# Weight loads of the retention stage: from SyncE's queue to ScalarE's

## The chip, the cores and the metric

The kernel runs on one core of one Trainium2 chip. What counts is the device time of one execution in microseconds (us); lower is better. Engines are named as the profile names them: PE (TensorE, the matrix multiplies; PEld its weight loads), DVE (VectorE), ACT (ScalarE), POOL (GpSimd) and SP (SyncE, which here only starts transfers). A transfer (DMA) is issued by one engine's instruction stream, stands in that engine's queue, and is carried out by 16 DMA engines that all queues share.

## The reference

Three blocks follow one another: a retention (linear attention with decay), a soft mixture of experts, and a two-layer MLP.

```python
# retention: q, k, v are (4, 8, 768, 64)
gamma = 1.0 - 2.0 ** (-5.0 - np.arange(H))
for t in range(S):
    state = gamma * state + einsum('bhd,bhe->bhde', k[:, :, t], v[:, :, t])
    y[:, :, t] = D ** -0.5 * einsum('bhd,bhde->bhe', q[:, :, t], state)
x = y as (3072 tokens, 512)
# soft mixture of experts: phi (512, 32), w1 (8, 512, 1024), w2 (8, 1024, 512)
logits = x @ phi
slot_input = softmax(logits, axis=0).T @ x
slot_out = relu(slot_input @ w1[e]) @ w2[e]          # per expert e, 4 slots each
x = softmax(logits, axis=1) @ slot_out
# MLP: w_in (512, 2048), w_out (2048, 512)
h = x @ w_in
out = (h * sigmoid(1.702 * h)) @ w_out
```

## The kernel before

The retention is computed in 24 chunks of 128 tokens (four batches of six chunks). For each chunk three tensors come from memory: `ktv` (512 KB: the transposed k and the plain v side by side), `qt` (256 KB, transposed q) and, for 12 of the chunks, `kt` (256 KB, plain k; the chunks in `KTP` get it from a transpose on PE, copied out by ACT at L222, and the last chunk of a batch needs none). Each has three buffers that are used in turn.

The loop over i (its body starts at L876) works on several chunks at a time. Iteration i does `stage_a(i)` (scores `sc`, L210, from q and k of chunk i), `stage_v(i)` (POOL scales v), `stage_b(i-1)` (output `y` from the state at L255 and from the scores at L259, then the new state `st` at L267, which ACT copies to `s_sb` at L269), `stage_c(i-2)` (a transpose `xp`, which ACT copies to `x` at L291). Every fourth iteration adds the logits of a group of four chunks and the copies of them on ACT (L337 to L321), the next one the group's first softmax steps.

Loads are issued in the same iteration: the halves of expert weights (below), `load_b(i+1)` for k, and `load_a(i+2)` for `ktv` and q of chunk i+2. The buffer of q that `load_a(i+2)` fills is that of chunk i-1, and its last reader is `y` at L255 in `stage_b(i-1)`. The whole program stands under a manual schedule: each engine runs its instructions in the order in which the code lists them, and SP does so too, so that it may run ahead of the others as far as its waits allow.

Expert weights are cut into 32 pieces of 1 MB. During the retention 17 of them are loaded, in 34 halves of 512 KB (`load_half`, L120), into buffers that nothing has used before (`wp` and `wq`; one of them held `ktv` of chunk 2). The loop issues three halves in iteration 1 and then one or two in each iteration up to 22, by `min(2 * (NW + NQ), 2 + i * 2 * (NW + NQ) // (NI - I0))` with NW + NQ = 17. The other 15 pieces are loaded behind the retention (`load_piece`, L136, and two halves), when buffers of the retention are free; their first users are the matrix multiplies `hp` (L488) and `eo` (L513).

All loads of the loop are issued by SP. ACT issues two loads of constants at the very start, POOL two more. SP's and ACT's issues together draw on eight completion semaphores in turn, in program order, so that each issue waits until the eighth one before it has landed.

Of the kernel before, what the change touches and what calls it, by code (L numbers as in the profile page):

```python
# [33 lines left out]
NW = 14  # L34
# [15 lines left out]
def retention_soft_moe_mlp(  # L50
# [13 lines left out]
    nc = tc.nc  # L64
# [3 lines left out]
    def pool(stack, name, bufs, **kw):  # L68
        e = ctx.enter_context(ExitStack())
        kw.setdefault("reuse_waits", "tile")  # L70
        if "space" not in kw:
            kw["side"] = "left" if stack is left else "right"
        t = e.enter_context(tc.tile_pool(name=name, bufs=bufs, **kw))
        return t, e
# [4 lines left out]
    wp, _ = pool(left, "wp", NW)  # L79
    sm, sm_e = pool(right, "sm", 2)  # L80
    xx, xx_e = pool(right, "xx", 5)
    wq, wq_e = pool(left, "wq", NQ)
# [34 lines left out]

    half = []

    def load_half(pool):  # L120
        if half:
            t, src = half.pop()
            nc.sync.dma_start(out=t[:, 2:4], in_=src[:, 2:4])
            return
        kind, e, k = pieces.pop()
        t = pool.tile([P, 4, 512], F32, tag="w", name=f"{kind}_{e}_{k}")
        src = (w1 if kind == "w1" else w2)[e, k].rearrange("p (j f) -> p j f", j=4)
        nc.sync.dma_start(out=t[:, 0:2], in_=src[:, 0:2])
        W[kind, e, k] = t
        half.append((t, src))  # L130

# [42 lines left out]
    def load_a(i):  # L174
        if i < NI:
            src = ktv[i].rearrange("p (a t) -> p a t", a=2)
            if i == 2:
                early.append(wp.tile([P, 4, 512], F32, tag="w", name="early"))
                ktv_t[i] = early[0][:, 0:2]
            else:  # L180
                ktv_t[i] = wt(f"ktv{i % 3}", [P, 2, 512], f"ktv{i}")
            if i < 2:
                nc.sync.dma_start(out=ktv_t[i][:, 0], in_=src[:, 0])
            else:
                nc.sync.dma_start(out=ktv_t[i], in_=src)
            qt_t[i] = wt(f"qt{(i + 1) % 3}", [P, NP, P], f"qt{i}")
            nc.sync.dma_start(out=qt_t[i], in_=qt[i].rearrange("p (a t) -> p a t", a=NP))
# [4 lines left out]
    def load_b(i):  # L192
        if i < NI and i % NC < NC - 1:
            if i == 3:
                t = early[0][:, i].rearrange("p (h d) -> p h d", h=H)
            else:
                t = wt(f"kt{(i - i // NC) % 3}", [P, H, D], f"kt{i}")
            if i not in KTP:
                nc.sync.dma_start(out=t, in_=kt[i].rearrange("p (h d) -> p h d", h=H))
            kt_t[i] = t  # L200
# [3 lines left out]
    def stage_a(i):  # L204
        q_, kv = qt_t[i], ktv_t[i]
        kT = kv[:, 0].rearrange("p (a t) -> p a t", a=NP)
        sc = [ps.tile([P, NP, P], F32, tag=f"sc{hh}", name=f"sc{hh}_{i}") for hh in range(2)]
        for a in range(NP):
            for hh in range(2):
                mm(sc[hh][:, a, :], lhsT=kT[hh * D:(hh + 1) * D, a, :], rhs=q_[hh * D:(hh + 1) * D, a, :],  # L210
                   start=True, stop=True)
        pt = [wt(f"pt{hh}{i % 2}", [P, NP, P], f"pt{hh}_{i}") for hh in range(2)]
        for hh in range(2):
            nc.vector.tensor_tensor(  # L214
                out=pt[hh], in0=sc[hh], in1=mask[:, None, :].to_broadcast([P, NP, P]), op=ALU.mult
            )
        p_t[i] = pt
        if i in KTP and i % NC < NC - 1:
            kp = ps.tile([P, NP, P], F32, tag="m", name=f"kp{i}", bufs=3)
            for a in range(NP):  # L220
                nc.tensor.transpose(kp[:, a, :], kT[:, a, :], ident)
            nc.scalar.copy(out=kt_t[i].rearrange("p h d -> p (h d)"), in_=kp.rearrange("p a t -> p (a t)"))  # L222

    def stage_v(i):
        c = i % NC
        v_ = ktv_t.pop(i)[:, 1].rearrange("p (h d) -> p h d", h=H)
        vt = wt(f"vt{i % 2}", [P, H, D], f"vt{i}")
        nc.gpsimd.tensor_tensor(
            out=vt, in0=v_, in1=vs[:, c, :, None].to_broadcast([P, H, D]), op=ALU.mult
        )  # L230
        vt_t[i] = vt
        if c == 0:
            tb_t[i] = tab
        else:
            tb_t[i] = wt("tb", [P, NP, P], f"tb{i}")
            nc.gpsimd.tensor_tensor(
                out=tb_t[i], in0=tab, in1=gsc[:, :, c, None].to_broadcast([P, NP, P]), op=ALU.mult
            )
# [3 lines left out]
    def stage_b(i):  # L242
        c = i % NC
        q_, vt, pt = qt_t.pop(i), vt_t.pop(i), p_t.pop(i)
        y = ps.tile([P, 2, 512], F32, tag="y", name=f"y{i}")

        def out_(a, hh):
            o = hh ^ (a & 1)
            return y[o * D:(o + 1) * D, a % 2, P * (a // 2):P * (a // 2) + P]

        if c > 0:
            for a in range(NP):
                for hh in range(2):
                    r = slice(hh * D, (hh + 1) * D)
                    mm(out_(a, hh), lhsT=s_sb[r, a, :], rhs=q_[r, a, :], start=(a < 2), stop=False,  # L255
                       skip_group_check=True)
        for a in range(NP):
            for hh in range(2):
                mm(out_(a, hh ^ (a & 1)), lhsT=vt[:, 2 * a + (hh ^ (a & 1)), :], rhs=pt[hh ^ (a & 1)][:, a, :],  # L259
                   start=(c == 0 and a < 2), stop=True, skip_group_check=True)  # L260
        if c < NC - 1:
            if c == 0:
                st_p[0] = ps.tile([P, NP, D], F32, tag="st", name=f"st{i}")
            st, k_ = st_p[0], kt_t.pop(i)
            for a in range(NP):
                for hh in range(2):
                    mm(st[hh * D:(hh + 1) * D, a, :], lhsT=k_[:, 2 * a + hh, :], rhs=vt[:, 2 * a + hh, :],  # L267
                       start=(c == 0 and a == 0), stop=True, skip_group_check=True)
            nc.scalar.copy(out=s_sb, in_=st)  # L269
        xT = xx.tile([P, NP, P], F32, tag="xT", name=f"xT{i}")  # L270
        nc.vector.tensor_tensor(
            out=xT.rearrange("p (s k) t -> p k s t", k=2), in0=y[:, :, 0:2 * P].rearrange("p k (s t) -> p k s t", s=2),
            in1=tb_t.pop(i).rearrange("p (s k) t -> p k s t", k=2), op=ALU.mult,
        )
        xT_t[i] = xT

    def stage_c(i, split=False):
        xp = ps.tile([P, DM], F32, tag="m", name=f"xp{i}", bufs=3)
        for a in range(NP):
            nc.tensor.transpose(xp[:, a * P:(a + 1) * P], xT_t[i][:, a, :], ident)  # L280
        x_t[i] = xp
        if not split:
            stage_c2(i)
# [15 lines left out]
    def stage_g1(g, part=False):  # L299
        if part in (True, False):  # L300
            lp = logits(g)
            if part:
                return lp
        else:
            lp = part
        softmax_stats(g, lp)
# [547 lines left out]
    with tc.manual_schedule():  # L854
# [18 lines left out]
        loaded = 0  # L873
        ex_t = {}
        for i in range(NI + 2):
            if i == 2:  # L876
                stage_b(1)
            if i < NI:
                stage_a(i)
                stage_v(i)  # L880
                while i > 0 and loaded < min(2 * (NW + NQ), 2 + i * 2 * (NW + NQ) // (NI - I0)):
                    load_half(wp if loaded < 2 * NW else wq)
                    loaded += 1
                load_b(i + 1)
                load_a(i + 2)
            if i >= 8 and i % 4 == 0 and i < NI:
                ex_t[i // 4 - 2] = row_softmax(i // 4 - 2)
            if i >= 9 and i % 4 == 1 and i < NI:
                row_norm(i // 4 - 2, ex_t.pop(i // 4 - 2))
            if 1 <= i <= NI and i != 2:  # L890
                stage_b(i - 1)
            if i >= 2:
                n = i - 1
                g = n // 4 - 1
                if i < NI + 1:
                    stage_c(i - 2)
                else:
                    lp = stage_g1(g, True)
                    stage_c(i - 2, True)
                    softmax_stats(g, lp)  # L900
                    combine1()
                    last_z = stage_g2(g)
                    stage_c2(i - 2)
                if n % 4 == 0 and i <= NI:
                    stage_g1(g)
                if n % 4 == 1 and n > 4:
                    stage_g2(g)
                if n % 4 == 2 and 4 < n < 22:
                    stage_g3(g)
# [337 lines left out]
```

## Time and profile before

| | before |
|---|---|
| median of 3 runs | 450.64 us (448.06 to 453.56) |
| the profiled execution | 451.76 us |
| its span | 450.0 us |
| PE busy | 433.1 us (96% of the span) |
| DVE, ACT, POOL busy | 333.4, 205.3, 47.9 us |
| moved by DMA | 92.38 MB, 79.16 MB read from memory |
| q1, the queue of nearly all transfers | 27248 packets, 91.24 MB |

The retention takes the first 109 us or so of the span. The span is the time from the first to the last instruction; the rest of an execution's time lies around it. PE's granted clock is 0.999 of full speed in this execution. A busy share is an average over the span; what ends a wait in one stage is read from that stage.

### The profile page before, as it was taken

The numbers are of one execution on the slowest core, as the hardware profiler recorded it, in microseconds if no ns is written. First come the engines' busy times: TensorE is split into PE (matmuls) and PEld (weight loads), VectorE is DVE, ScalarE is ACT, GpSimd is POOL, SyncE is SP. The second block draws the span as 40 slices with busy tenths as digits, with TensorE's granted clock in tenths as the row PEclk, the third lists the DMA queues.
The fourth block names the chain that finished last, engine by engine and source line by source line (L and its number), as shares of the span: only waits on it lengthen the run. The fifth ranks groups of instructions, "written<-read, shape, count | busy, mean of one in ns | idle before, by whom it ended". The sixth has DMA issues, their size and how long they took to land.

```text
span 450.0 us, 9917 instructions
## 1 busy us (share of the span) xinstructions
PE 433.1 (96%) x4105; PEld 359.9 (80%) x4105; DVE 333.4 (74%) x600; ACT 205.3 (46%) x351; POOL 47.9 (11%) x53
## 2 busy tenths in 40 slices
PE   8799998999999989999999999999999999999996
PEld 5687876877533367788888889999999999999995
DVE  2345665756456587987979689897797797988984
ACT  2232232322220166474656655655555555565530
POOL 3353543343100000000000000000000000000000
PEclk9999999999999999999999999999999999999999
DMA  8999999999899968687555502001301401311012
GB/s 300 407 365 408 389 371 407 344 407 325 328 411 411 380 228 281 182 299 268 181 194 188 184 5 94 1 1 47 129 14 47 141 1 49 140 48 46 23 74 93
DMA packets 27661, 92.38 MB, mean 205 GB/s; under 512 B 2864, under 2 KB 4288, under 8 KB 23264
## 3 DMA queue, kind: packets, MB, share of 16 engines
q1 hardware_dynamic: 27248, 91.24, 55.1%
q8 instruction: 32, 0.52, 0.5%
q10 hardware_dynamic: 288, 0.36, 0.3%
q0 software_dynamic: 80, 0.15, 0.1%
q14 instruction: 13, 0.11, 0.1%
HBM read 79.16 MB, written 12.58 MB: 204 GB/s over the span
## 4 chain that ended last, share of the span: by engine, by line
PE 81%; DMA 12%; DVE 3%; ACT 1%; issue 1%; POOL 1%; SPq 0%; DVEq 0%; POOLq 0%; ACTq 0%
PE P L730 35%; PE acc L667 18%; DMA qt<-qt_dram 10%; PE sc L210 4%; PE hb L696 4%; PE hp L488 3%; PE y L259 3%; PE eo L513 3%; PE y L255 2%; PE P L840 2%; PE xp L280 1%; PE op L370 1%; PE h L644 1%; DMA ktv_first<-ktv_dram 1%; PE st L267 1%
## 5 line engine op out<-in xcount | busy, mean ns | idle before, releaser
L691 DVE TENSOR_TENSOR forms<-forms 128x256 f32<-128x256 f32 (+1 forms) x93 | 47.6, 512 | 22.3 <-ACT forms L698 21.0
L698 ACT ACTIVATE forms<-hb 128x512 f32<-128x512 f32 x62 | 37.2, 599 | 54.7 <-PE hb L696 34.9
L667 PE MATMUL acc<-wo_hl,gh 128*128 128x512 f32 x192 | 59.8, 394 | 0.4 <-ACT gh L646 0.4
L730 PE MATMUL P<-bh,la 128*128 128x256 f32 x208 | 59.0, 284 | 0.0
L730 PE MATMUL P<-bl,ha 128*128 128x256 f32 x208 | 58.8, 283 | 0.0
L730 PE MATMUL P<-bh,ha 128*128 128x256 f32 x208 | 58.7, 282 | 0.0
L214 DVE TENSOR_TENSOR pt<-sc,ca_t 128x512 f32<-128x512 f32 x44 | 28.3, 685 | 24.5 <-PE sc L210 24.5
L730 PE MATMUL P<-bh,hs 128*128 128x256 f32 x156 | 44.1, 283 | 0.0
L730 PE MATMUL P<-bh,ls 128*128 128x256 f32 x156 | 44.1, 282 | 0.0
L730 PE MATMUL P<-bl,hs 128*128 128x256 f32 x156 | 44.0, 282 | 0.0
L667 PEld LDWEIGHTS acc<-wo_hl,gh 128*128 128x128 f32 x192 | 35.4, 188 | 8.1 <-issue 0.6
L730 PEld LDWEIGHTS P<-bl,ha 128*128 128x128 f32 x208 | 39.4, 189 | 1.2
L730 PEld LDWEIGHTS P<-bh,ha 128*128 128x128 f32 x208 | 39.4, 190 | 0.0
L730 PEld LDWEIGHTS P<-bh,la 128*128 128x128 f32 x208 | 39.4, 189 | 0.1
L691 DVE TENSOR_TENSOR la<-forms,ha 128x1024 fp32r<-128x1024 f32 x31 | 37.9, 1223 | 0.0
L667 PE MATMUL acc<-wo_hl,gl 128*128 128x512 f32 x96 | 37.4, 394 | 0.3 <-DVE gl L654 0.3
L714 ACT CAST ha<-forms 128x1024 fp32r<-128x1024 f32 x31 | 32.6, 1053 | 6.5 <-DVE forms L691 5.6
L646 ACT ACTIVATE gh<-h 128x512 fp32r<-128x512 f32 x30 | 18.0, 601 | 33.0 <-PE h L644 24.2
L714 ACT CAST hs<-forms 128x768 fp32r<-128x768 f32 x31 | 26.0, 839 | 10.1 <-DVE forms L691 7.5
L730 PEld LDWEIGHTS P<-bl,hs 128*128 128x128 f32 x156 | 29.5, 189 | 1.2
L210 PEld LDWEIGHTS sc<-qt,ktv 64*128 64x128 f32 x320 | 19.6, 187 | 13.1 <-issue 9.2
L210 PE MATMUL sc<-qt,ktv 64*128 64x128 f32 x320 | 23.2, 284 | 6.6 <-DMA qt<-qt_dram 6.6
(224 smaller groups left out, 925.2 us busy)
## 6 DMA issues: line engine op xcount, KB each, us to landing
w<-w_dram SPq DMA_DIRECT2D x36, 512.0 KB, 7.7
w<-w_dram SPq DMA_DIRECT2D x14, 1024.0 KB, 8.3
ktv<-ktv_dram SPq DMA_DIRECT2D x20, 512.0 KB, 8.3
wi<-w_in_dram SPq DMA_DIRECT2D x7, 1024.0 KB, 5.5
wo<-w_out_dram SPq DMA_DIRECT2D x7, 1024.0 KB, 4.9
parts<-stage SPq DMA_DIRECT2D x24, 256.0 KB, 2.9
pt<-parts SPq DMA_DIRECT2D x6, 1024.0 KB, 4.8
qt<-qt_dram SPq DMA_DIRECT2D x21, 256.0 KB, 6.5
```

What stands on the lines that cost most here:

```text
L210: mm(sc[hh][:, a, :], lhsT=kT[hh * D:(hh + 1) * D, a, :], rhs=q_[hh * D:(hh + 1) * D, a, :], start=True, stop=True)
L214: nc.vector.tensor_tensor(out=pt[hh], in0=sc[hh], in1=mask[:, None, :].to_broadcast([P, NP, P]), op=ALU.mult)
L259: mm(out_(a, hh ^ (a & 1)), lhsT=vt[:, 2 * a + (hh ^ (a & 1)), :], rhs=pt[hh ^ (a & 1)][:, a, :], start=(c == 0 and a < 2), stop=True, ski ...
L488: mm(hp[32 * j:32 * j + 32, :], lhsT=slotT[:, k, SPE * (j // 2):SPE * (j // 2) + NS], rhs=w[:, j, :], start=(k == 0), stop=(k == KDM - 1))
L513: mm(op[32 * j:32 * j + 32, :], lhsT=hT[:, kk, 32 * j:32 * j + 32], rhs=w[:, j, :], start=(kk == 0), stop=(kk == 3))
L646: nc.scalar.activation(out=gh, in_=hp, func=AF.Gelu_apprx_sigmoid)
L667: mm(acc[t], lhsT=g[:, t * P:(t + 1) * P], rhs=w, start=f == f0 and n == 0, stop=f == f1 and n == 2)
L691: nc.vector.tensor_tensor(out=out_, in0=a, in1=b_, op=op)
L696: mm(PB["h"], lhsT=gst[:, f * P:(f + 1) * P], rhs=cT[:, 512 * b:512 * b + 512], start=True, stop=True)
L698: nc.scalar.activation(out=t[:, 3 * a:3 * a + 2].rearrange("p s d -> p (s d)"), in_=PB["h"], func=AF.Gelu_apprx_sigmoid)
L714: nc.scalar.copy(out=AH[n, k], in_=FT[0][:, c0:c1])
L730: mm(PB[p][:, t], lhsT=g[:, c], rhs=w, start=r == span_[b][0] and t == 0 and i == 0, stop=r == span_[b][1] - 1 and i == 2, skip_group_chec ...
```

## The change

`load_half` gets a second argument, the engine that issues the load. The loop of the retention passes `nc.scalar`, so the 34 halves that it loads are issued by ACT, at the same place of the program. The two halves that are loaded behind the retention pass none and stay with SP, as do all loads of chunks. Sizes, buffers and order in the program are the same.

```diff
-    def load_half(pool):
+    def load_half(pool, q=None):
         if half:
             t, src = half.pop()
-            nc.sync.dma_start(out=t[:, 2:4], in_=src[:, 2:4])
+            (q or nc.sync).dma_start(out=t[:, 2:4], in_=src[:, 2:4])
             return
         kind, e, k = pieces.pop()
         t = pool.tile([P, 4, 512], F32, tag="w", name=f"{kind}_{e}_{k}")
         src = (w1 if kind == "w1" else w2)[e, k].rearrange("p (j f) -> p j f", j=4)
-        nc.sync.dma_start(out=t[:, 0:2], in_=src[:, 0:2])
+        (q or nc.sync).dma_start(out=t[:, 0:2], in_=src[:, 0:2])
...
                 while i > 0 and loaded < min(2 * (NW + NQ), 2 + i * 2 * (NW + NQ) // (NI - I0)):
-                    load_half(wp if loaded < 2 * NW else wq)
+                    load_half(wp if loaded < 2 * NW else wq, nc.scalar)
                     loaded += 1
```

## Rows read from the trace of the kernel before

**Rows 1.** Windows: stretch, length, busy us of engines, clock, DMA share, GB/s.

```profile
core 0: us, PE busy (x) PEld busy (x) DVE busy (x) ACT busy (x) POOL busy (x), PEclk, DMA share, GB/s
4.00:8.00 4.00, 3.97 (x24) 2.06 (x22) 0.59 (x1) 0.00 (x0) 0.00 (x0) 1.00 1.02 362
8.00:18.40 10.40, 7.99 (x124) 6.77 (x124) 4.66 (x8) 2.99 (x6) 6.19 (x6) 1.00 1.03 410
...
72.10:90.60 18.50, 17.47 (x302) 14.01 (x302) 11.15 (x23) 5.33 (x14) 7.32 (x8) 1.00 1.01 370
...
125.00:150.00 25.00, 25.00 (x220) 8.66 (x216) 15.82 (x54) 3.75 (x7) 0.95 (x1) 1.00 1.01 413
```

**Rows 2.** DMA view, all queues, 18.4 to 109 us.

```profile
DMA packets 11744, 34.88 MB, mean 385 GB/s; under 512 B 1302, under 2 KB 1302, under 8 KB 11656
```

**Rows 3.** Waits of PE, 0 to 125 us: total us, times, longest.

```profile
PE sc L210 <- DMA qt<-qt_dram: 6.6, 6, 1.8
...
PE y L255 <- ACT s_sb L269: 0.5, 1, 0.5
```

**Rows 4.** Chain of waits: start us, us, what; transfers of q.

```profile
9.95 8.45 DMA qt<-qt_dram
...
46.56 7.25 DMA qt<-qt_dram
...
101.19 7.78 DMA qt<-qt_dram
```

**Rows 5.** Lines L187 at 5.1, L136 at 120.4, L187 to 125 us, each with landings.

```profile
L187 SPq DMA_DIRECT2D qt_first<-qt_dram x1: 524/524/524, 5.1 to 5.1; - x1
...
DMA to landing us min/median/max: 5.9/5.9/5.9
...
L136 SPq DMA_DIRECT2D w<-w_dram x1: 327/327/327, 120.4 to 120.4; - x1
...
DMA to landing us min/median/max: 4.8/4.8/4.8
...
L187 SPq DMA_DIRECT2D qt<-qt_dram x21: 327/328/664, 9.9 to 101.2; - x21
...
DMA to landing us min/median/max: 4.1/6.4/8.4
```

**Rows 6.** DMA issues, 0 to 109 us: count, KB each, median us to landing.

```profile
w<-w_dram SPq DMA_DIRECT2D x34, 512.0 KB, 7.6
ktv<-ktv_dram SPq DMA_DIRECT2D x20, 512.0 KB, 8.3
qt<-qt_dram SPq DMA_DIRECT2D x21, 256.0 KB, 6.5
kt<-kt_dram SPq DMA_DIRECT2D x12, 256.0 KB, 7.9
```

**Rows 7.** Timeline of SP: start us, us, what.

```profile
5.92 0.33 SPq L128 DMA_DIRECT2D w<-w_dram  x1
...
9.58 0.33 SPq L185 DMA_DIRECT2D ktv<-ktv_dram  x1
...
101.57 0.43 SPq L123 DMA_DIRECT2D w<-w_dram  x1
```

**Rows 8.** Waits of SP's queue, 0 to 110 us: total us, times, longest.

```profile
SPq L187 <- PE y L255: 36.6, 17, 4.1
...
SPq L185 <- POOL vt_first L228: 1.1, 1, 1.1
```

**Rows 9.** Timeline of ACT: start us, us, what, idle before it.

```profile
10.53 0.59 ACT L222 COPY kt_first<-kp 128x512 f32<-128x512 f32 x1 [1.94 <-PE kp L221]
12.03 0.37 ACT L269 COPY s_sb<-st 128x256 f32<-128x256 f32 x1 [0.91 <-PE st L267]
...
99.48 0.59 ACT L291 COPY x<-xp 128x512 f32<-128x512 f32 x1
...
105.47 0.25 ACT L321 COPY lT<-lp 128x128 f32<-128x128 f32 x1
```

## The prediction, made before the changed kernel was run

> **What bounds the kernel now.** The change touches only loads of the retention, the first 109 us, so I read that stretch. First the table of windows, cut where PE waited [rows 1]. The reader is to see two columns. PE is busy nearly all the time (17.47 of 18.50 us in 72.1 to 90.6). The DMA share stands at 1.01 to 1.03 in every window, so the 16 engines never ran dry; at their best they move 410 GB/s here and 413 GB/s in 125 to 150 us, and over 18.4 to 109 us they moved 34.88 MB at a mean of 385 [rows 1, 2].
>
> Then PE's waits: six waits of `sc` (L210) for a q load, 6.6 us in all, the longest 1.8; one of 0.5 for `s_sb` [rows 3]. Nothing else stops PE. The chain of waits shows the six loads: each took 7.25 to 8.45 us from issue to landing. The first is that of chunk 3 (issued 9.95, landed 18.40), the last that of chunk 23 (issued 101.19, landed 108.97), and they come four chunks apart [rows 4].
>
> Why does a 256 KB load take that long? At 410 GB/s it is 0.64 us of transfer, a 512 KB load 1.28. A 1 MB load issued at 120.4 us, after a pause of the queue, landed in 4.8 us; less 2.56 of transfer that leaves 2.2 us fixed [rows 5]. So an undisturbed q load would land after 2.2 + 0.64 = 2.8 us; the shortest here took 4.1, the median 6.4 [rows 5]. Ahead of every q load stood 1.3 to 5.6 us of other transfers, half of them weights: 34 halves of 512 KB beside 20 `ktv` loads, 21 q loads and 12 k loads [rows 6].
>
> It looks as if putting the weights elsewhere would return 6.6 us. The test is what rate that takes. After chunk 3 PE waits 6.6 - 1.8 = 4.8 us in the 90.6 us from 18.4 to 109. To do without, the DMA engines must move the same 34.88 MB in 85.8 us: 407 GB/s throughout, against 385 measured and 410 at best. The window from 72.1 to 90.6 ran at 370 [rows 1]. So PE and DMA are nearly balanced, and the slower of the two is DMA. What is moved is the same after the change.
>
> **The change part by part.** *SP loses 34 issues*, some 0.33 to 0.43 us each [rows 7]. That is worth nothing by itself: what SP mostly waits for is a buffer (36.6 us for `y` L255, which frees q's) [rows 8].
>
> *ACT gains 34 issues.* At SP's 0.43 that is 14.6 us. In iteration i they stand behind the copies of iteration i-1 (and the `kt` copy of i, where there is one) and ahead of `s_sb`. That is where ACT idles. The tightest place is iteration 1 with three halves: the copy before them starts at 10.53, `s_sb` at 12.03 after 0.91 us of idle [rows 9]; 3 x 0.43 = 1.29 ends at 11.82. Cost 0. Were this cover gone everywhere, `s_sb` would be late, then `y` L255, then the release of q's buffer: up to 14.6 us; I keep this only as a bound. The halves write buffers that nothing used before (one was used up to chunk 3), so ACT waits for no release. It does wait for landings: SP and ACT draw on eight completion semaphores in turn, so each issue waits for the landing of the eighth before it. For a half that is a load of about two iterations earlier, some 9 us (chunks 3 to 23 took 90.6); a half lands after 7.6 at the median [rows 6]. So I take 0, with 1 us where one is late; queued behind it would be `s_sb` and the copy of x. By the same count SP's chunk loads come to wait for a half in seven places.
>
> *The first halves start later.* Today SP issues three from 5.92 on, and they fill the engines until the next `ktv`, which is held to 9.58 by POOL's reading of its buffer [rows 7, 8]. From ACT they come only after 10.53. The last load before them, q of chunk 2, lands at 5.1 + 5.9 = 11.0 [rows 5]; into an empty queue the `ktv` of 9.58 lands at 9.58 + 2.2 + 1.28 = 13.1, where it would have been 11.0 + 1.28 = 12.3 without a gap. The engines lose 0.8 us; where they set the end, so does the kernel. (Bounds: 0, if chunks still have slack there, and 1.5.) Chunk 3 itself gains: its q lands near 13.7 instead of 18.40, and 1.8 us of waiting goes. But the weights that stood ahead of it have yet to be moved, and the wait is back four or eight chunks later.
>
> *Order at the end.* All that a second queue can give is to have weights still under way when the last chunk's q lands. Now one half is behind it (issued 101.57) [rows 7]. Program order makes ACT issue those of iteration 21 after the copy at 99.48 and the last after that of 105.47 [rows 9]. So q of chunk 23 can pass two more at best: -2.6 us. If the queues share evenly, the chunk loads of that iteration (k 0.64, ktv 1.28, q 0.64) and its two halves (2.56) come to the same and finish together: 0; and the last half may slow q by 0.6. I take 0.
>
> *A rule against it.* The rows say that the engines, not the issuing, are full. The Trainium skill, DMA: Bandwidth & Descriptors, section "Issuing engines are not separate DMA queues", says that DMAs started from several engines run on the same 16 DMA engines and that only issue time is saved. By that alone the sum would be 0, by the rows +0.8.
>
> *Behind the retention* PE is without a gap (25.00 of 25.00 us in 125 to 150) [rows 1], and its late weight loads are issued as PE frees buffers, so a shift of the retention's end passes through whole.
>
> **Sum.** 451.76 us (span 450.0 and 1.76 around it) + 0.8 = 452.6. That execution is 1.1 above the median of the runs, 450.64, so 451.4.
>
> **Rivals.** *Chunk loads pass the weights.* If the queues are served in turn and the weights fall behind, a q load waits for `ktv` and k alone, lands 3 to 5 us after issue, and the six waits go: 450.64 - 6.6 + 0.8 = 444.8. For it: the six waits are all on q. Against it: the rate of 407, and that weights can fall behind by no more than the two halves above. Beside this stands the Trainium skill, DMA: Bandwidth & Descriptors, section "Queues, rings and completion order", by which each engine takes packets from its queues in turn; no run here shows two loaded queues for long.
>
> *The engines run dry (slower).* ACT issues a half later than SP does. In the iterations behind a group's logits (6, 10, 14, 18, 22) by some 4 us: 105.5 against 101.57 [rows 7, 9]. The median backlog of 3.6 us (6.4 - 2.8) is about that. If the queue empties each time for one half, 5 x 1.28 = 6.4, with the 0.8 about 457.8. Against it: SP, rid of the halves, issues k and ktv earlier and fills the gap. It decides if the mean rate of 18.4 to 109 us falls from 385 below 368 (4.5 us more).
>
> *Two queues move less.* The only stretch with several queues loaded, 4 to 8 us, ran at 362 GB/s instead of 410 [rows 1]. If all of the retention lost these 12%, 101 us would become 114: +13, 464. That is also the stretch in which the first loads of all start up, so I take no loss; a third of it would be 4.5.
>
> **How the numbers follow.** About 1% (4.5 us) is what a measurement here tells from no change. Forecast 0.72 (448 to 454); passing 0.10; dry 0.10; less rate 0.08. Faster 0.10 is the passing case. Slower 0.14: about 0.07 each of the last two; their mild forms stay within 1%, which makes 0.76. The range, 447.5 to 455.5, holds the forecast with its -2.6 and the 2.6 us that runs scatter, and the mild forms of the last two; the full rivals lie outside.
>
> **What the profile of after would show.** Right: the DMA share stays at 1.0 from 8 to about 109 us with a mean near 385 GB/s; PE's waits for q stay at 4 to 7 us, with none at chunk 3; ACT's idle before `s_sb` shrinks by the issues and `s_sb` is not late. Wrong: waits for q gone and `hp` (L488) starting 5 us or more earlier (passing); windows with DMA share under 0.9 (dry); share 1.0 but under 370 GB/s (less rate); PE waiting for `s_sb` (ACT held up).

## The result, and the profile after

| | before | after |
|---|---|---|
| median of the runs | 449.62 us (448.06 to 454.89, 18 runs) | 454.17 us (450.99 to 459.14, 18 runs) |
| ratio of after to before | | 1.0085 (95% interval 1.0061 to 1.011) |
| profiled execution, its span | 451.76, 450.0 us | 454.57, 452.8 us |
| last q load landed (issue plus time to landing, from the trace) | 108.97 us | 110.76 us |

The changed kernel is 0.85% slower, 3.8 us on 450: inside 1%, but a real loss. The ratio leaves out single executions that lie far above the fastest of their kernel and is not the quotient of the two medians, which lie 4.55 us apart. The prediction of 451.4 (0.8 us slower than before) had the sign and a fifth of the size.

First the windows of after, in the columns of [rows 1].

```profile
8.00:18.40 10.40, 9.62 (x144) 8.00 (x142) 5.25 (x8) 2.99 (x6) 6.14 (x6) 1.00 0.91 313
18.40:36.00 17.60, 15.58 (x288) 13.06 (x285) 7.67 (x14) 3.98 (x10) 6.15 (x6) 1.00 1.03 406
36.00:53.80 17.80, 15.40 (x262) 12.41 (x265) 9.64 (x21) 5.11 (x14) 7.17 (x7) 1.00 0.96 352
53.80:72.10 18.30, 17.31 (x302) 13.81 (x294) 10.90 (x25) 5.53 (x16) 7.20 (x8) 1.00 1.03 398
72.10:90.60 18.50, 18.50 (x336) 15.06 (x330) 11.66 (x25) 5.69 (x16) 8.19 (x8) 1.00 0.98 368
8.00:109.00 101.00, 92.71 (x1584) 75.45 (x1580) 55.78 (x111) 28.58 (x73) 42.03 (x41) 1.00 0.99 376
```

Before, two of the same windows that [rows 1] leaves out, and the whole stretch:

```profile
36.00:53.80 17.80, 17.34 (x302) 14.15 (x302) 11.01 (x23) 5.36 (x14) 7.31 (x8) 1.00 1.03 402
53.80:72.10 18.30, 17.04 (x286) 13.62 (x286) 10.60 (x23) 5.67 (x16) 7.97 (x9) 1.00 1.00 378
8.00:109.00 101.00, 93.62 (x1609) 76.48 (x1609) 56.84 (x114) 29.88 (x76) 43.32 (x43) 1.00 1.02 388
```

The mean rate fell from 388 to 376 GB/s. Before moved 388 x 101 us = 39.2 MB here; at 376 that takes 104.2 us, 3.2 more. The first window lost most: 313 GB/s against 410 [rows 1], (410 - 313) x 10.4 us = 1.01 MB, 2.5 us at 400 GB/s. From 18.4 on after moved 383 GB/s, before 385 [rows 2], but that mean hides two things: up to 36 us after moved 406 GB/s against 381 and gave back 0.44 MB, and from 36 to 109 us it moved 378 against 386 and lost another 0.58 MB, 1.5 us. Two loaded queues are not slow in themselves: at a share of 1.03 they moved 398 and 406 GB/s. The window that is low against before is that of 36 to 53.8 us (352 against 402), with a share of 0.96; the 368 of 72.1 to 90.6 are no loss, since before moved 370 there [rows 1].

PE's waits of after, 0 to 130 us (total, times, longest), beside [rows 3]:

```profile
PE sc L210 <- DMA qt<-qt_dram: 6.7, 7, 1.3
...
PE y L255 <- ACT s_sb L269: 1.2, 2, 0.8
```

The waits for q neither went nor grew in sum. As forecast, the one at chunk 3 went (its q was issued at 10.22 and landed at 13.88, not 18.40). They came back elsewhere, as the chain of waits shows beside [rows 4]:

```profile
20.45 7.73 DMA qt<-qt_dram
34.92 8.16 DMA qt<-qt_dram
49.49 7.18 DMA qt<-qt_dram
...
129.36 14.44 DMA w<-w_dram
143.82 15.32 DMA w<-w_dram
```

The last two rows are new: late weights behind the retention, which add some 0.5 us (`hp` starts 2.27 us later than before, the span is 2.8 longer). The last q landed only 1.79 us later than before. PE came to it 0.57 us after it had landed, where before PE had waited for it, so the other 0.5 us ahead of `hp` is PE's own lag from earlier waits.

### The profile page after: what moved, and what is told of

Its sections match the earlier page's. It is cut to its first block, busy times and chain, and to the rows that moved or that the text cites. A ratio compares the mean times of both kernels' runs of the same rounds, so it can differ in the third digit from the quotient of the medians.

```text
span 452.8 us, 9915 instructions
## 1 busy us (share of the span) xinstructions
PE 435.3 (96%) x4105; PEld 360.6 (80%) x4105; DVE 333.5 (74%) x600; ACT 205.1 (45%) x351; POOL 47.8 (11%) x53
## 4 chain that ended last, share of the span: by engine, by line
PE 80%; DMA 15%; DVE 3%; ACT 1%; issue 1%; DVEq 0%; ACTq 0%
PE P L730 34%; PE acc L667 17%; DMA qt<-qt_dram 8%; DMA w<-w_dram 7%; PE sc L210 5%; PE hb L696 4%; PE y L259 3%; PE y L255 2%; PE P L840 2%; PE xp L280 2%; PE st L267 1%; PE h L644 1%; PE wu L870 1%; PE lp L312 1%; PE hp L488 1%; PE kp L221 1%
## 5 line engine op out<-in xcount | busy, mean ns | idle before, releaser
L730 PEld LDWEIGHTS P<-bh,hs 128*128 128x128 f32 x156 | 29.5, 189 | 0.0
L691 DVE TENSOR_TENSOR ls<-forms,hs 128x768 fp32r<-128x768 f32 x31 | 29.5, 951 | 0.0
```

The costliest lines, as they stand in the source:

```text
L691: nc.vector.tensor_tensor(out=out_, in0=a, in1=b_, op=op)
L730: mm(PB[p][:, t], lhsT=g[:, c], rhs=w, start=r == span_[b][0] and t == 0 and i == 0, stop=r == span_[b][1] - 1 and i == 2, skip_group_chec ...
```

## The experiments

All twelve are told. Edits stand against the changed kernel unless said otherwise; "halves" are the 34 weight loads of 512 KB. The letters in the expectations are theories of their time; what became of each stands below it. One plain note on e1: its profiled execution took 457.18 us against a median of 452.27, so its trace is not a typical one.

**Halving the change.** The first three halves on SP and the rest on ACT (e1), and the reverse (e2).

```diff
-  load_half(..., nc.scalar)
+  load_half(..., nc.sync if i == 1 else nc.scalar)   # e1
+  load_half(..., nc.scalar if i == 1 else nc.sync)   # e2
```

> The three halves of iteration 1 are issued by SP again, as before the change; the other 31 by ACT. Theory A (the late first halves leave the DMA engines idle near 10 us, and that is nearly the whole loss): the stretch 8 to 18.4 us moves about 410 GB/s again, instead of 313, and the time is within 1 us of before (ratio 0.998 to 1.003). Theory B (ACT's later issues let the engines run dry again and again through the retention): windows with a low rate at 45, 50 and 83 us stay, and most of the 3.8 us stays (ratio 1.005 to 1.009). Theory C (two loaded queues move less): as B, but with the DMA share at 1.0 and a mean rate under 385 GB/s in all windows.

> The reverse: only the three halves of iteration 1 are issued by ACT, the other 31 by SP. Theory A: 2 to 4 us slower than before (ratio 1.004 to 1.009), with the low rate in 8 to 18.4 us and none behind it. Theory B: 0.5 to 1.5 us slower, the idle near 10 us alone (1.001 to 1.003). Theory C: as before (0.999 to 1.001).

Measured: e1 1.0039 (1.001 to 1.0067), 1.8 us; e2 1.0052 (1.0024 to 1.0079), 2.3 us. The two add up to the 3.8 of the whole within their intervals. So the loss has two parts, the three halves that start late and the other 31; which is the larger these intervals don't tell. Of the ranges only A's for e2 held: A missed e1 by 0.1%, B missed both, and C wanted e2 as before. The first window of e2 shows the first part, that of e1 its absence:

```profile
8.00:18.40 10.40, 9.54 (x143) 8.03 (x141) 5.03 (x8) 2.99 (x6) 6.15 (x6) 1.00 0.94 315
```

```profile
8.00:18.40 10.40, 9.62 (x144) 8.05 (x142) 5.25 (x8) 2.99 (x6) 6.15 (x6) 1.00 1.03 407
```

The second part shows in the windows of 36 to 109 us: e2, with the other 31 halves on SP, moved 386 GB/s there, as before did, and after 378. The 1.5 us that this is worth are near e1's 1.8.

**Is it lateness, or the other queue?** In e3 ACT issues the halves one place earlier, behind the chunk loads of the iteration before, which is the order that SP had. In e4 SP alone issues everything, with the halves late, behind the chunk loads of their iteration.

```diff
-  while i > 0 and loaded < min(..., 2 + i * ...): load_half(..., nc.scalar)
   load_b(i + 1)
   load_a(i + 2)
+  while loaded < min(..., 2 + (i + 1) * ...): load_half(..., nc.scalar)   # e3
+  while i > 0 and loaded < min(..., 2 + i * ...): load_half(...)          # e4
```

> All 34 halves are issued by ACT, but each one iteration earlier in the program, behind the chunk loads of that iteration; the first three come behind the first kt copy of ACT (about 8 us) instead of the second. If lateness of ACT's issues is the cause (theories A and B), both the gap near 10 us and the dry stretches go, and the time is that of before or a little less (ratio 0.994 to 1.002). If two loaded queues move less (theory C), or ACT is held up by its issues, it stays slower by 3 us or more (1.006 and over).

> All halves on SP's queue as before the change, but behind the chunk loads of their iteration instead of ahead of them, so that they are issued about as late as ACT issues them after the change, the first three near 10.5 us. Theories A and B (lateness): slower than before by 1 to 4 us (ratio 1.002 to 1.009) with one queue alone. Theory C, or ACT held up: as before (0.998 to 1.002).

Measured: e3 1.0162 (1.0127 to 1.0198), 7.3 us slower; e4 0.9949 (0.9928 to 0.9969), 2.3 us faster. The lateness theories (A and B) wanted 0.994 to 1.002 for e3 and 1.002 to 1.009 for e4, and missed both. SP's old order, on the second queue, costs twice what the change does, and later halves on one queue are a gain: lateness as such isn't the cause. e4's whole stretch ran at 386 GB/s, hardly other than before; what it gains is at the end. Where before has one half behind the last q, e4 has three (its SP timeline):

```profile
100.48 0.33 SPq L187 DMA_DIRECT2D qt<-qt_dram  x1
100.86 0.42 SPq L123 DMA_DIRECT2D w<-w_dram  x1
101.33 0.42 SPq L128 DMA_DIRECT2D w<-w_dram  x1
102.03 1.04 SPq L123 DMA_DIRECT2D w<-w_dram  x1
```

Two more of 1.28 us each are 2.6 us; 2.3 was measured, and PE's waits for q fell from 6.6 to 2.5 us. That fits the "order at the end" of the prediction, bound -2.6. Two queues reach the same order (e11 and e12 below have three halves behind the last q as well), but there the gain is lost again by a lower rate.

**Is it the completion semaphores?** SP and ACT share eight of them in turn. In e5 ACT issues 17 whole pieces instead of 34 halves; in e6 POOL issues the halves, on semaphores of its own.

```diff
-  load_half(..., nc.scalar); loaded += 1
+  load_piece(..., "w", nc.scalar); loaded += 2   # e5
+  load_half(..., nc.gpsimd); loaded += 1         # e6
```

> As after the change, but ACT issues whole pieces (17 loads of 1 MB) instead of 34 halves. SP and ACT then take 77 completion semaphores instead of 94 in the retention, so a load waits for one that is further back. Theory L (the eight semaphores in turn tie the two queues together, and engines run dry because a load waits for an older one of the other queue): the time comes nearer to before (ratio 1.000 to 1.005). Theory S (chunk loads lose their place before the weights because two queues are served side by side; what is issued later is moved at the same time): a piece of 1 MB beside a q load takes more from it, so no better than after (1.008 to 1.015).

> As after the change, but POOL issues the 34 halves; its loads have eight completion semaphores of their own, so SP's chunk loads no longer wait for halves, nor halves for chunk loads. POOL's own work (two scalings a chunk) stands around them, and one of its issues took 0.5 to 0.7 us at the start. Theory L: faster than after, ratio to before 0.996 to 1.004. Theory S: still a second queue beside SP's, so as slow as after or slower (1.006 to 1.015).

Measured: e5 1.014 (1.0083 to 1.0198), e6 1.0087 (1.0051 to 1.0124). Half as many draws on the semaphores didn't help, and POOL, apart from them, loses as much as ACT. So the shared semaphores are not the cause (theory L falls), nor is ACT's other work by itself. The traces agree: from 8 us to the last q no load of e5 or e6 was issued right behind the landing of the eighth before it. Why whole pieces lose more than halves isn't explained. e6's profiled execution took 452.10 us, the fastest of its runs (median 454.96), so it stands in no table here.

**How far does the one queue carry?** e7 is e4 with the halves one iteration later still; e8 is e4 with the first three left where they were.

```diff
   load_b(i + 1); load_a(i + 2)
-  while i > 0 and loaded < min(..., 2 + i * ...): load_half(...)           # e4
+  while i > 0 and loaded < min(..., 2 + (i - 1) * ...): load_half(...)     # e7
+  # e8: as e4, but for i == 1 the while stands ahead of load_b and load_a
```

> One queue (SP), halves behind the chunk loads as in e4_sp_late, and one more iteration later, so that four or five halves instead of three stand behind the last q load. Theory D (in one queue the end of the retention is set by the bytes that stand before the last q): another 1.28 us for each half that moves behind it, up to what PE still waits (2.5 us in e4): ratio 0.989 to 0.993. If e4's gain was only that q goes ahead of the halves of its own iteration, the same as e4 (0.994 to 0.996).

> As e4_sp_late, but the three halves of iteration 1 stand ahead of the chunk loads again, issued near 6 us as before the change. If the gap near 10 us costs what it leaves unmoved (about 0.7 MB, 1.7 us), this is faster than e4_sp_late by 1 to 2 us (ratio to before 0.990 to 0.993). If the gap costs nothing in one queue, because chunk 3 gets its loads sooner, it is the same as e4 or slower (0.994 to 0.998).

Measured: e7 0.9943 (0.9916 to 0.9969), e8 0.9939 (0.9905 to 0.9973). Both are as e4 within their intervals, so the further gain of still later halves (D) isn't seen, though one more half behind the last q, 0.3%, would be too little to tell. Nor could the late start, 2.3 us in e2, be told in one queue with late halves (e4 against e8, 0.1% apart). e4, e7 and e8 beat both kernels, by 2.3 to 2.7 us. In e8's profiled execution PE was busy 98.96 of 101 us, so there is next to nothing left for loads to give back in this stretch:

```profile
8.00:109.00 101.00, 98.96 (x1703) 80.81 (x1702) 59.68 (x117) 30.80 (x78) 44.85 (x44) 1.00 1.02 395
```

**Turn it round: the urgent load on the second queue.** Weights, `ktv` and k stay on SP; q of chunk i + 2 is issued by ACT behind `s_sb` of chunk i - 1. e9 is that edit on the kernel before, e10 on e4.

```diff
   def load_a(i): ...
-      nc.sync.dma_start(out=qt_t[i], ...)
   ...
   if 1 <= i <= NI and i != 2:
       stage_b(i - 1)
+  load_q(i + 2, nc.scalar)      # q's buffer and load; q of chunks 0 and 1 stay on SP
```

> The kernel before with one load of each chunk moved: the q loads of chunks 2 to 23 (256 KB each) are issued from ScalarE's queue, behind s_sb of the chunk whose buffer they take; ktv, k and all weight halves stay on SyncE's in their old order. Again two queues, but now the urgent small load has one for itself, and the bulk is together in the other. Theory S (a load shares with what the other queue holds, so it loses its place if the bulk is issued elsewhere): here the sharing works for q: it lands 3.5 to 5 us after issue at the median (6.5 before, 7.0 after the change), PE's waits for q fall below 3 us, some of it comes back as waits for ktv or k, since the same bytes have to be moved; ratio 0.985 to 0.997. Rival T (two loaded queues cost the engines rate, whatever is in them): q may land sooner, but the DMA share or the rate of 8 to 109 us falls as after the change (0.99, 376 GB/s against 1.02, 388) and the ratio is 1.004 to 1.02.

> The same with the order of the one-queue kernel that issues its halves behind the chunk loads of their iteration (e4, 0.9949): q loads from ScalarE's queue, all else from SyncE's, halves last in their iteration. Theory S: nothing is lost against e4, ktv comes earlier as well, ratio 0.985 to 0.995. Rival T: e4's gain is lost again to the second queue, ratio 1.0 to 1.012.

Measured: e9 1.0317 (1.0248 to 1.0385), e10 1.0445 (1.0398 to 1.0493): the worst two of all, 14 and 20 us. All ranges missed, T's too. Theory S falls here. Its claim that a load shares at once with what the other queue holds would have brought q in 3.5 to 5 us; with a queue for itself it took nearly as long as ever (DMA issues of e9's page; 6.5 in [rows 6]):

```profile
qt<-qt_dram ACTq DMA_DIRECT2D x21, 256.0 KB, 6.2
```

Loads did overtake: within SP's queue none ever landed before an earlier one, but in e9 q loads landed ahead of loads that SP had issued before them, by up to 2.3 us (q issued at 17.09 landed at 23.50, `ktv` issued at 16.24 landed at 25.78). That is too little to shorten q's median by more than 0.3 us. So in these traces a load waits for most of what is already under way, whichever queue that came from. And theory T's plain form falls too: with both queues loaded the first window of e9 ran at full rate.

```profile
8.00:18.40 10.40, 8.55 (x128) 7.05 (x127) 5.18 (x8) 2.99 (x6) 6.15 (x6) 1.00 1.03 411
```

One place where e9 loses is 38 to 50 us. ACT issues q late (chunk 3's at 12.56 us, where SP had issued it at 9.95 [rows 4]); that of chunk 7, issued at 35.54, landed at 43.43, and PE waited 3.10 us for it. While PE waited, no buffer came free, SP issued nothing from 38.58 to 47.80, ACT's next q stood until 47.94 behind a copy of `s_sb` that waited 6.76 us for PE, and the engines ran empty. PE itself ran at half its clock from 44 to 47 us (the third number from the end), which lengthened the standstill. Timeline of SP, then the windows:

```profile
38.58 0.43 SPq L128 DMA_DIRECT2D w<-w_dram  x1
47.80 0.33 SPq L204 DMA_DIRECT2D kt<-kt_dram  x1
```

```profile
44.00:45.00 1.00, 1.00 (x13) 0.81 (x10) 0.00 (x0) 0.00 (x0) 0.00 (x0) 0.55 0.40 158
45.00:46.00 1.00, 1.00 (x12) 0.97 (x12) 0.92 (x2) 0.00 (x0) 0.00 (x0) 0.50 0.16 57
46.00:47.00 1.00, 1.00 (x14) 1.00 (x12) 0.37 (x1) 0.00 (x0) 0.00 (x0) 0.50 0.03 12
```

**The last place on ACT.** e11 puts ACT's halves behind `s_sb` of chunk i - 1, so behind the chunk loads as in e4; e12 also leaves the first three on SP in their old place.

```diff
-  while i > 0 and loaded < ...: load_half(..., nc.scalar)      # e11
+  while i == 1 and loaded < ...: load_half(...)                # e12
   load_b(i + 1); load_a(i + 2)
   ...
   if 1 <= i <= NI and i != 2:
       stage_b(i - 1)
+  while 0 < i < NI and loaded < ...: load_half(..., nc.scalar)
```

> The changed kernel with ScalarE's halves one place later in its program: those of iteration i behind s_sb of chunk i - 1 instead of ahead of it, so behind the chunk loads of their iteration, as in e4, but on the second queue. With e3 (earliest place on ScalarE, 1.0162) and the change (middle place, 1.0085) that makes three places on the same queue. Theory O (landings follow the order of issue whichever queue a load is in; in all traces with two queues few loads overtook one of the other queue; what costs is bulk that is issued ahead of a q load because ScalarE does not stand still where SyncE waits for q's buffer): this place is like e4, q's waits fall below 5 us, ratio 0.995 to 1.002, lower than the change's. Rival T (two loaded queues cost rate whatever the order): 1.006 to 1.016. Rival E (what costs is that the engines empty while ScalarE is held up, and then take some us to come back to 400 GB/s): still later issue empties them more often, windows with a DMA share under 0.95 in the middle of the retention, ratio 1.006 or more.

> The same with the first three halves on SyncE ahead of the chunk loads, as before the change, so that the engines do not empty at 9 to 11 us. Theory O: 0.99 to 1.0, within 0.4% of e11, as e8 stood to e4. Rival T: about 0.3% below e11, 1.003 to 1.013. Rival E: the start is repaired, 8 to 18.4 us at 405 to 411 GB/s as before, and e12 is 0.4 to 0.6% faster than e11; emptied engines later in the retention remain, ratio 1.002 or more.

Measured: e11 1.0073 (1.0037 to 1.011), e12 1.005 (1.002 to 1.008). Theory O (order of issue alone) wanted 0.995 to 1.002 and 0.99 to 1.0 and falls: with e4's order, and three halves behind the last q as there, ACT's queue is 1.2% slower than SP's. By the ratios T and E are both left; e12 is 0.23% faster than e11, where E wanted 0.4 to 0.6 and T about 0.3, and the intervals don't tell these apart. The windows speak for E, the engines that empty. In e12 the start is repaired (8 to 18.4 us at 407 GB/s), from 36 to 109 us its two queues moved 383 GB/s, close to the 386 of before, and most of what it moved less lies at one place:

```profile
20.00:21.00 1.00, 1.00 (x8) 0.77 (x6) 0.65 (x2) 0.00 (x0) 0.00 (x0) 0.50 0.83 330
21.00:22.00 1.00, 1.00 (x18) 0.54 (x16) 0.64 (x2) 0.57 (x1) 0.00 (x0) 0.69 0.06 25
22.00:23.00 1.00, 1.00 (x22) 0.96 (x20) 0.00 (x0) 0.02 (x1) 0.00 (x0) 1.00 0.05 20
23.00:24.00 1.00, 1.00 (x24) 0.88 (x18) 0.69 (x1) 0.30 (x1) 0.00 (x0) 1.00 0.82 176
```

Its timelines, SP and then ACT, show that both queues stood still together, SP for q's buffer and ACT behind a copy that waited for PE.

```profile
14.60 0.43 SPq L185 DMA_DIRECT2D ktv_first<-ktv_dram  x1
22.18 0.33 SPq L187 DMA_DIRECT2D qt<-qt_dram  x1
```

```profile
15.86 0.33 ACTq L123 DMA_DIRECT2D w<-w_dram  x1
...
21.43 0.59 ACT L222 COPY early<-kp 128x512 f32<-128x512 f32 x1 [4.50 <-PE kp L221]
23.70 0.37 ACT L269 COPY s_sb<-st 128x256 f32<-128x256 f32 x1 [1.68 <-PE st L267]
23.72 0.33 ACTq L128 DMA_DIRECT2D w<-w_dram  x1
```

PE was late for two reasons: it had waited 2.02 us for q of chunk 3, and then ran at half its clock (0.50 in the row of 20 to 21 us), so that the score multiplies took 2.08 us, as in e3 below. In e4 and e8 the clock stayed at 1.00. So what separates ACT's late place from SP's is emptied engines and a lower clock together; what each is worth wasn't taken apart.

**One sum for all.** In each of the fourteen traces the span is the landing of the last q plus 340.6 to 342.4 us. That landing follows from two readings: the mean rate of 8 to 109 us, and how many halves land behind the last q. This is a sum of what was moved when; why the rates differ it doesn't say.

| kernel | halves behind last q | GB/s, 8 to 109 | last q landed, us | ratio |
|---|---|---|---|---|
| before | 1 | 388 | 108.97 | 1 |
| after | 1 | 376 | 110.76 | 1.0085 |
| e2 | 1 | 382 | 110.44 | 1.0052 |
| e3 | 0 | 366 | 116.02 | 1.0162 |
| e4 | 3 | 386 | 106.55 | 0.9949 |
| e8 | 3 | 395 | 104.22 | 0.9939 |
| e9 | 0 | 343 | 123.70 | 1.0317 |
| e11 | 3 | 364 | 111.34 | 1.0073 |
| e12 | 3 | 372 | 108.34 | 1.005 |

For e8 it works out like this: 39.2 MB less two halves of 0.52 are 38.2; at 395 GB/s 96.6 us, so q at 104.6 (104.22 seen). For e9: 39.2 + 0.52 at 343, 115.8, so 123.8 (123.70 seen). After, e11 and e12 come out 1.5, 1.5 and 2.3 us too late, since their rate differs on the two sides of the last q. The rates are of single executions, so a difference of a few GB/s between two rows says little.

## Why the prediction was right or wrong

*What bounds the kernel: right in the main.* The end follows the landing of the last q in every kernel (table above). In seven of the fourteen traces, after's among them, PE came to that q's chunk 0.35 to 1.5 us after it had landed, so there earlier waits of PE set the last bit. What the prediction passed over is that full engines need not be fast ones. Its DMA share of 1.01 to 1.03 in every window leaves out the 1.00 of 53.8 to 72.1 us, and in before's own rows a share near 1 goes with rates far below 410 GB/s:

```profile
80.00:86.00 6.00, 6.00 (x126) 5.24 (x126) 3.45 (x9) 2.23 (x5) 2.46 (x3) 1.00 0.95 308
83.00:84.00 1.00, 1.00 (x27) 0.83 (x18) 1.00 (x3) 0.00 (x0) 0.45 (x1) 1.00 1.06 293
```

A q load that seemed dear for its 8 us was a symptom, and taking the weights off its queue moved the waits without shortening them (6.7 us in sum).

*SP loses 34 issues, worth nothing: right.* Only chunk 3's q landed earlier, and that because no halves stood ahead of it (it was issued at 10.22 us, before at 9.95).

*ACT gains 34 issues, cost 0: wrong, the step that failed.* I costed what the issues do to ACT's own work, and that was about right: `y` waited 1.2 us for `s_sb`, 0.7 more than before, for the landing of a half behind which `s_sb` stood. What I took for 0 was the reverse, what ACT's waits for PE do to the transfers. e1 sizes it: 1.8 us (0.5 to 3.0), and the 378 GB/s of after from 36 to 109 us, against e2's 386, agree with that. That all of it comes from ACT's waits isn't shown. A place in after is at 45 us: neither queue issued anything from 41.21 to 45.00, since SP waited for q's buffer and ACT stood before a copy from PE (ACT's timeline, then windows).

```profile
44.99 0.58 ACT L222 COPY kt<-kp 128x512 f32<-128x512 f32 x1 [2.28 <-PE kp L221]
45.00 0.34 ACTq L128 DMA_DIRECT2D w<-w_dram  x1
```

```profile
45.00:46.00 1.00, 1.00 (x25) 0.83 (x26) 0.97 (x4) 0.58 (x1) 0.00 (x0) 1.00 0.65 256
46.00:47.00 1.00, 1.00 (x30) 1.00 (x26) 0.38 (x2) 0.31 (x1) 0.00 (x0) 1.00 0.94 309
47.00:48.00 1.00, 1.00 (x15) 0.76 (x13) 0.50 (x1) 0.60 (x2) 0.42 (x1) 1.00 0.95 268
```

The kernel before moved 387 and 416 GB/s in the first two of these:

```profile
45.00:46.00 1.00, 1.00 (x22) 0.88 (x23) 0.07 (x1) 0.43 (x1) 1.00 (x2) 1.00 1.03 387
46.00:47.00 1.00, 1.00 (x26) 0.83 (x24) 1.00 (x2) 0.00 (x0) 0.70 (x1) 1.00 1.06 416
```

There SP had issued q at 42.80 and, with no wait between, two halves, k and `ktv` by 44.69. This is the rival "engines run dry" in a mild form: the mechanism holds, but the places are not the five I named, and its point of decision (a mean of 18.4 to 109 us under 368, which is worth 4.2 us and not the 4.5 stated) wasn't reached; it was 383. Two of its other signs came: windows with a share under 0.9, and PE waiting for `s_sb`.

*First halves start later, +0.8: right in kind, sized too small.* The gap came where it was forecast. e2 measured 2.3 us (1.1 to 3.6), beyond the bound of 1.5, though the interval doesn't exclude it. What I left out is that the engines didn't come back at full rate when work arrived:

```profile
9.00:11.00 2.00, 1.75 (x18) 1.44 (x19) 0.96 (x3) 0.56 (x1) 2.00 (x3) 1.00 0.76 266
11.00:13.00 2.00, 1.96 (x36) 1.66 (x35) 1.46 (x3) 0.59 (x1) 0.83 (x1) 1.00 0.94 338
13.00:17.00 4.00, 3.57 (x68) 3.21 (x69) 1.22 (x3) 0.74 (x2) 2.03 (x2) 1.00 0.89 271
```

At 400 GB/s the first of these lost 0.27 MB, 0.7 us: the term as I had it. The other two lost 0.12 and 0.52 MB, 1.6 us more. Why the return takes 6 us stays open. One queue has it too, in part less of it (e4: 340 GB/s from 11 to 13 us, 350 from 13 to 17), and it is not forecast by any row of before that I used. The engines are busy meanwhile (share 0.89 to 0.94), as before's are at 80 to 86 us (share 0.95, rows above), where no gap stands ahead, so a gap is not the only thing that lowers the rate.

*Order at the end, 0: right.* Only one half landed behind the last q in after, as before.

*Two queues move less: refuted as a rule* (398 to 411 GB/s with both loaded). *Chunk loads pass the weights: refuted*, most sharply by e9. The Trainium skill, DMA: Bandwidth & Descriptors, section "Queues, rings and completion order", has each engine take packets from its queues in turn; the overtaking told of at e9, by 2.3 us at most, fits that, but no run shows what an engine does with its queues. The same page's "Issuing engines are not separate DMA queues" says that only issue time is saved: the runs agree that nothing else is gained, and show what it doesn't speak of, a loss of 3.8 us.

*Sum:* 0.8 was forecast; the two parts measure 2.3 and 1.8, the whole 3.8. The chance for "within 1%" was right, near its edge. That 454.17 lies in the stated range is luck in part: the range had been widened for mild forms of the two slower rivals, while the sum itself had the second part at 0.

Open: why two issuing engines empty the DMA engines more often than one, in general. At 21 us in e12, 45 in e9 and 45 in after it is shown what each queue stood for; that ACT's earliest place (e3) is its worst isn't explained (its clock at half, below, is a part). A kernel with the halves on an engine that never waits for PE wasn't run (POOL, in e6, scales v and so waits for loads and buffers too).

## What to carry to other kernels

Where the DMA engines nearly set the end, as here, don't expect a second queue to move bytes sooner: bulk loads put on a compute engine's queue are issued when that engine's waits allow, and both queues can then stand still at once. Try first to keep urgent and bulk loads in one queue and to work on their order: bulk behind the urgent loads of its step, and as much of it as may be behind the very last urgent one (e4: 0.9949 with the same bytes). Read an emptied queue from windows of 1 to 2 us, since long ones average it away, and look some microseconds past the gap before you cost it. A DMA share near 1 doesn't say that the rate is at its best; read the GB/s beside it.

## What the runs showed of the hardware that was not expected

In after, a gap was followed by 6 us at 271 to 338 GB/s, though the DMA share was back at 0.9 (the rows of 9 to 17 us above): 0.7 us of gap came to 2.3. Over the kernels, e3 aside: the five without a gap near 10 us (before, e1, e8, e9, e12) moved 406 to 412 GB/s from 11 to 17 us. Of the eight with a share of 0.57 to 0.83 from 9 to 11 us, seven moved 289 to 347 there (shares of 0.81 to 1.00), on one queue (e4, e7) or two, but e5, with its 1 MB loads, 403. So the slow return goes with the gap in most kernels and not in all, and low rates without a gap exist as well (before at 80 to 86 us).

In some kernels PE's granted clock fell to half while PE waited for a load. In e3 PE waited 4.08 us for q of chunk 3 and then ran at 0.50 until 26 us (PE's timeline, then windows; the clock is the third number from the end):

```profile
20.86 2.08 PE L210 MATMUL sc<-qt,ktv 64*128 64x128 f32 x16 [4.08 <-DMA qt<-qt_dram]
```

```profile
20.00:22.00 2.00, 1.14 (x10) 1.17 (x12) 0.00 (x0) 0.40 (x1) 0.22 (x1) 0.50 0.94 332
22.00:24.00 2.00, 2.00 (x18) 1.44 (x18) 1.06 (x2) 0.19 (x1) 0.00 (x0) 0.50 0.73 246
24.00:26.00 2.00, 2.00 (x26) 1.67 (x28) 0.23 (x1) 0.59 (x1) 0.00 (x0) 0.50 0.93 320
```

0.50 is the lower of its two levels, 1.2 GHz. The 16 score multiplies took 2.08 us there and 1.16 at full clock (27.55 us). So this late load was paid twice, and a slower PE frees buffers later, which fits the DMA share of 0.73. In after the longest wait for q was 1.3 us and the clock stayed at 1.00 in the windows shown, so this is no part of the 2.8 us of its profiled execution. The clock fell to half in e1, e5 and e9 to e12 too; in e2 it stayed at 1.00 through a wait of 2.4 us, so the length of the wait alone doesn't tell. In the kernels where it fell, how much of the loss is the clock's wasn't taken apart.
